# The seam between two layers: last rows in halves of tokens, a table fetched sooner, one W2 piece in a slot of its own

## The chip, the cores and the metric

The kernel runs on one core of a Trainium2 chip. TensorE (PE) multiplies, VectorE (DVE), ScalarE (ACT) and GpSimd (POOL) do the element-wise work, and the queues of SyncE (SP), ACT and POOL issue transfers to 16 DMA engines. The metric is the device time of one execution in microseconds (us).

## The reference

Two layers, each made of a spectral part A and a dense part B, both on a residual of 2048 tokens by 1024 features:

```python
x = A_x
x = x + _A_ref(_layernorm(x, axis=-1), A_w_r, A_w_i)
x = x + _B_ref(_layernorm(x, axis=-1), B_w1, B_b1, B_w2)
x = x + _A_ref(_layernorm(x, axis=-1), A_w_r, A_w_i)
x = x + _B_ref(_layernorm(x, axis=-1), B_w1, B_b1, B_w2)
```

`_A_ref` is a real 2-D FFT over tokens and features, a multiplication by the complex filter `w_r + i w_i`, and the inverse FFT. `_B_ref` is `act(x @ w1 + b1) @ w2` with 3584 hidden features and the activation h * tanh(softplus(h)), which ScalarE has as Mish.

## The kernel before, in words

Everything is written out by hand: each engine has its own list of instructions (`Prog`), in the order in which the Python code adds them, and each buffer (`Res`) remembers which counts of which semaphores its readers and writers must have reached. A transfer's waits are on the queue of the engine that issues it, so a waiting transfer holds back all that follows on that queue. On-chip memory is one big tensor, ARENA, in which `alloc` places named buffers at fixed offsets; a buffer laid over an older one inherits the older one's readers and writers as waits.

The residual stands in XS as 16 tiles j of 128 tokens. Layer A wants it in another order, XR: 128 rows, one for each (j, h) of token tile and feature block, each with 128 tokens n by 128 features. Its stages are: `s1` (L636), 16 groups of 8 matmuls, group j over tokens n = 8j to 8j + 7 of XR, each group read out of PSUM by ACT (L642) or DVE (L644) into Y; then by frequency group g = 0 to 7, in an order written out in `order_A`: `s2` (L726), `s3` (L771 to L774, then the filter's multiplications on DVE, L782 to L789, with the filter WT and the table FT), `i1` (L800, table BT), `i2` (L825). Tables FT and BT have rings of three buffers, filter groups a ring of eight buffers, two for each group. In layer 0 the filter is made and written to DRAM (`w_scratch`); in layer 1 it is read back by `load_w` on POOL's queue.

Layer B works by 512 hidden or output columns with a seven-product scheme. The second matmul of a pair of token blocks (`products`) has seven stages n, each with one block of W2 (or of sums of its blocks) and four token tiles t; a `tile_product` is 14 matmuls (L1309), seven for each of two pieces k of the W2 block. In the last pass of layer 0 the stages are in the order `BACK`, so that the residual's tiles become final one after the other in stages 4 and 6: (4, t) gives tile 12 + t, and (6, t) gives tile 8 + t. `turn_of` ends with (5,0), (5,1), (5,2), (6,0), (6,1), (6,2), (5,3), (6,3). W2 pieces are 896 KB and live in four slots R0 to R3:

```python
PB[n][k] = load_w2(stages[n][1], k, f"R{(2 * n + k + 1) % 4}")
```

They are loaded when stage n - 2 is over. So the two pieces of stage 6 (the block B21) take R1 and R2 after stage 4, while stage 5 uses R3 and R0.

At the seam each finished tile of the residual is normalised by DVE (L524) and goes to XR. All tiles but the last go by way of DRAM: `xn_store` on POOL's queue, `xr_load` on SP's. The last one, j = 11, is copied straight from the tile into XR by `xr_direct`, one copy for each of the eight feature blocks h, over the queues POOL, ACT, SP, POOL in turn. Meanwhile TensorE runs 38 filler matmuls (`spin`, L653). The residual's other data dependences at the seam are `r_xr`, two resources of 64 tokens each: `xr_load` and the whole-token `xr_direct` write both.

The next layer's tables and filter are opened by `open_tables(1)` ahead of `products`: filter groups 0 to 3, then FT and BT of groups 0 and 1, all on POOL's queue. The filter's eight buffers are the last 16 KB of ARENA. The slots WS0 to WS2 of the first matmul's weights end in the same place; WS2 is the last 7 KB.

Of the kernel before, what the change touches and what calls it, by code (L numbers as in the profile page):

```python
# [180 lines left out]
class KB:  # L181
# [185 lines left out]
    def layout(self):  # L367
        K = 1024
        self.o = dict(XR=0, Z=0, X=12 * K, T=20 * K, YK=28 * K, V=40 * K, JT=48 * K, M0=49 * K, IDF=49 * K + 256, RT=50 * K,
                      JUNK=51 * K, WR=54 * K, YS=96 * K, UT=64 * K, MN=64 * K, Y=96 * K, XN=128 * K, U=128 * K,  # L370
# [285 lines left out]
    def ring(self, name, n, size, shape):  # L656
        return [self.alloc(f"{name}{i}", self.o[name] + size * i, shape) for i in range(n)]

    def open_tables(self, li):

        self.li = li
        self.WT = self.ring("WT", 8, 2048, [2, 512])
        self.FTr = self.ring("FT", 3, 1536, [2, 384])
        self.BTr = self.ring("BT", 3, 1536, [2, 384])
        if li == 0:
            self.WR = self.ring("WR", 2, 4096, [2, 2, 512])
        for g in range(2 if li == 0 else 4):
            self.load_w(g)
        for g in range(2):
            self.load_tabs(g, li == 0)  # L670
            self.load_btabs(g, li == 0)

    def load_tabs(self, g, sp=False):
        b = self.FTr[g % 3]
        self.dma(self.sp if sp else self.pool, b.ap, self.con["FT"][g], f"ft{g % 3}{sp}", writes=[b.res])
# [10 lines left out]
        off = (self.o["WT"] + 2048 * i) // 2  # L686
        return self.ARENA[:, off:off + 2048].rearrange("p (a b c) -> p a b c", a=2, b=2)

    def load_w(self, g):
        if self.li == 0:  # L690
            self.load_wr(self.wr(g), g)
            return
        i = 2 * g % 8
        self.dma(self.pool, self.wt_pair(i), self.w_d[g], f"wt{g % 4}", reads=[self.r_wd[g]], writes=[w.res for w in self.WT[i:i + 2]])

    def layer_A(self, li):
        if li == 0:
# [6 lines left out]
        dve, act, sp, pool = self.dve, self.act, self.sp, self.pool  # L704
        ring, load_tabs, load_btabs, load_w = self.ring, self.load_tabs, self.load_btabs, self.load_w
        WT, FT, BT = self.WT, self.FTr, self.BTr
# [3 lines left out]
        def filter_bins(g):  # L710
            ps, banks, _ = self.pair()
            self.filter_bins(g, ps, banks, self.wr(g), WT[2 * g % 8:2 * g % 8 + 2], o["WT"] + 2048 * (2 * g % 8),
                             self.JT, self.r_jt, dve)

        def zslot(g, i):
            return Z[(2 * g + i) % 6]

        def s2(g, half):
# [14 lines left out]
            else:  # L733
# [16 lines left out]

            zz = self.ARENA[:, o["Z"] // 2 + (2 * g % 6) * K:o["Z"] // 2 + (2 * g % 6 + 2) * K].rearrange(
                "p (s r k) -> p s r k", s=2, r=2)
# [12 lines left out]
        def s3(g, i):  # L765

            ps, banks, _ = self.pair()
            z, ft = zslot(g, i), FT[g % 3]
            t = ft.ap[:, i, :]
            fns = [  # L770
                lambda e: e.matmul(ps[:, 0:512], t[:, 0:128], z.ap[:, 0, :], start=True, stop=False),  # L771
                lambda e: e.matmul(ps[:, 512:1024], t[:, 0:128], z.ap[:, 1, :], start=True, stop=False),
                lambda e: e.matmul(ps[:, 512:1024], t[:, 128:256], z.ap[:, 0, :], start=False, stop=True),
                lambda e: e.matmul(ps[:, 0:512], t[:, 256:384], z.ap[:, 1, :], start=False, stop=True),  # L774
            ]
            self.group(fns, reads=[z.res, ft.res], writes=banks)
            x = X[(2 * g + i) % 4]
            self.op(act, lambda e: e.activation(x.ap.rearrange("p a b -> p (a b)"), ps, ACT.Copy, scale=SIG),  # L778
                    reads=banks, writes=[x.res])
            wt, yk = WT[(2 * g + i) % 8], YK[(2 * g + i) % 6]  # L780
            ta, tb = T[2 * i], T[2 * i + 1]
            self.op(dve, lambda e: e.tensor_tensor(ta.ap, x.ap, wt.ap[:, 0:1, :].to_broadcast([P, 2, 512]), ALU.mult),  # L782
                    reads=[x.res, wt.res], writes=[ta.res])
            self.op(dve, lambda e: e.tensor_tensor(tb.ap, x.ap, wt.ap[:, 1:2, :].to_broadcast([P, 2, 512]), ALU.mult),
                    reads=[x.res, wt.res], writes=[tb.res])
            yk.res.begin()
            self.op(dve, lambda e: e.tensor_tensor(yk.ap[:, 0, :], ta.ap[:, 0, :], tb.ap[:, 1, :], ALU.subtract),
                    reads=[ta.res, tb.res], parts=[yk.res])
            self.op(dve, lambda e: e.tensor_tensor(yk.ap[:, 1, :], tb.ap[:, 0, :], ta.ap[:, 1, :], ALU.add),  # L789
                    reads=[ta.res, tb.res], parts=[yk.res])  # L790
# [117 lines left out]
                back((act, sp)[q % 2], 1, q, 1)  # L908

        self.s1(li)  # L910
        Z = ring("Z", 6, 2 * K, [2, 512])
        X = ring("X", 4, 2 * K, [2, 512])
        T = ring("T", 4, 2 * K, [2, 512])
# [8 lines left out]
        for stage, g, h in self.order_A():  # L922
            if stage == 2:
                s2(g, h)
                if li == 0 and h == 0:
                    filter_bins(g)
                    if g in (0, 1):
                        load_w(g + 4)
                    elif g in (4, 5):
                        load_w(g + 2)  # L930
            elif stage == 3:
                s3(g, h)
                if h:
                    if g < 6:
                        load_tabs(g + 2)
                    if li == 0:
                        self.keep_filter(g)
                    elif g < 4:
                        load_w(g + 4)
            elif stage == 4:  # L940
                i1(g, h)
                if h and g < 6:
                    load_btabs(g + 2)
            else:
                i2(g, h)
                u_turn(g, h)
# [160 lines left out]
    def layer_B(self, li, last):  # L1107
        pe, dve, act, sp, pool = self.pe, self.dve, self.act, self.sp, self.pool
# [164 lines left out]
        PB = [[None, None] for _ in range(7)]  # L1273
# [4 lines left out]
        def load_w2(name, k, slot, prog=sp):  # L1278

            b = self.alloc(f"W2{slot}", SLOT[slot], [7, 512])  # L1280
            f = slice(7 * k, 7 * k + 7)
            if name in T_OF:
                src, reads = self.w2s_d[T_OF[name]][:, f, :], [self.r_w2d[T_OF[name]][k]]
            else:
                d = 512 * int(name[2]) - 512
                src, reads = w2o[int(name[1]) - 1][:, f, d:d + 512], []
            self.dma(prog, b.ap, src, f"w2{slot}{prog.name}", reads=reads, writes=[b.res])
            return b

        STD = (("A11", "B11", 0, True), ("A12", "B21", 0, False), ("S", "T3", 1, True), ("A21", "T1", 0, True), ("A11", "T2", 1, True),  # L1290
               ("S", "B22", 0, False), ("A22", "T4", 1, False))
# [3 lines left out]
        def load_b(stages, n, k):  # L1295
            PB[n][k] = load_w2(stages[n][1], k, f"R{(2 * n + k + 1) % 4}")
# [20 lines left out]
        def products(p, s_off, stages, extra, loads=True):  # L1317
# [83 lines left out]
            for n, t in turn_of:  # L1401
                a, b, g, start = stages[n]
                bank = sets[g][t]
                if n or t:
                    tile_product(n, t, bank, ap[a], lambda k: part(a, k), start)
                after(b, t, bank)
                for f, k in sums.get((n, t), ()):
                    f(k)
                if t == 3 and n < 5 and loads:
                    for k in range(2):  # L1410
                        load_b(stages, n + 2, k)
                extra(n, t)

        self.xn_ring()
# [98 lines left out]
        gate = Res("gate")  # L1513
# [141 lines left out]
        stages = STD if last else BACK  # L1655
# [22 lines left out]
        def extra(n, t):  # L1678
            if last:
                return  # L1680
            if (n, t) == (2, 0):
                self.warm(ACT.Sqrt)
            if (n, t) == (3, 3):
                self.open_xr()
                for j in range(8):
                    self.xr_load(j)
            if n == 5 and t < 3:
                self.xr_load(12 + t)
            if (n, t) == (5, 2):
                self.xr_load(15)  # L1690
            if n in (4, 6):
                j = 4 * (n == 4) + 8 + t
                self.stats_second(j, 0, False)
                self.root(j, 1)
                b = self.apply(j, out=True)
                if j == 11:
                    self.xr_direct(j, b, 1, (pool, act, sp, pool))
                else:
                    self.xn_store(j, b)
            if n == 6 and t < 3:  # L1700
                if t:
                    self.xr_load(7 + t)
            if (n, t) == (5, 3):
                self.xr_load(10)
# [41 lines left out]
```

## Time and profile before

| | |
|---|---|
| median of three executions | 936.67 us (935.53 to 938.5) |
| profiled execution | 935.49 us, span 933.7 us |
| granted TensorE clock, mean | 0.993 |
| TensorE matmuls, busy share of the span | 94% |
| stage products and seam of layer 0 to 1 | about 397 to 500 us of the span |

Times in the views are microseconds from the start of the span. A line of the timeline gives the start, the length from the first to the last instruction of a run of equal ones, the engine, the source line, the operation with what it writes and reads, and the number of instructions; in square brackets, how long the engine stood idle before and what released it. A line of the waits gives the waiting engine and line, what it waited for, microseconds in total, the number of times, and the longest. The chain that ended last runs from the last instruction back through what released each step. "Issue" is time in which nothing that the profile shows was waited for. SPq, ACTq and POOLq are the queues' own work of issuing.

### The profile page before, as it was taken

What the parts mean: (1) busy time and instruction counts of PE and PEld (TensorE: products, weight loads), DVE (VectorE), ACT (ScalarE), POOL (GpSimd) and SP (SyncE); (2) the same over time, 40 slices, a digit from 0 to 9 for tenths busy, and PEclk for the clock granted to TensorE, in tenths of its full rate; (3) what the DMA queues carried; (4) which work ended last, traced back from release to release, by engine and by line L of the source; (5) the groups of instructions that cost most, each with busy time, mean ns of one, the idle gap of its engine ahead of it and who ended that gap; (6) DMA issues with size and microseconds to landing.
All of it is one profiled execution on the core that took longest, in us unless ns stands there. A gap on an engine that the chain in (4) does not pass through costs nothing.

```text
span 933.7 us, 13542 instructions
## 1 busy us (share of the span) xinstructions
PE 875.4 (94%) x5479; PEld 469.9 (50%) x5479; DVE 620.2 (66%) x985; ACT 434.4 (47%) x641; POOL 157.3 (17%) x181
## 2 busy tenths in 40 slices
PE   0699799999999999999999987999999999999998
PEld 0577486444444444444447765764444444444443
DVE  6698468687789667568756865666747665554473
ACT  6798485456213485420009975847650015552000
POOL 3923003960003641010120200000000000000000
PEclk9999989999999999999999998999999999999999
DMA  8969861674787388364830796445166635832432
GB/s 268 264 233 299 216 182 56 237 277 122 275 257 246 136 316 294 122 235 144 295 112 32 226 228 152 159 148 168 57 192 191 198 125 195 278 119 80 170 124 111
DMA packets 147392, 175.99 MB, mean 188 GB/s; under 512 B 68617, under 2 KB 125961, under 8 KB 147209
## 3 DMA queue, kind: packets, MB, share of 16 engines
q1 hardware_dynamic: 134656, 128.78, 44.7%
q0 software_dynamic: 10608, 44.70, 13.4%
q10 hardware_dynamic: 2064, 1.64, 0.6%
q8 instruction: 43, 0.70, 0.3%
q14 instruction: 21, 0.16, 0.1%
HBM read 130.78 MB, written 40.89 MB: 184 GB/s over the span
## 4 chain that ended last, share of the span: by engine, by line
PE 82%; DVE 6%; DMA 6%; ACT 4%; POOL 1%; issue 1%; SPq 1%; ACTq 0%; DVEq 0%; POOLq 0%
PE PS L1309 35%; PE PS L1210 29%; PE PS L1170 6%; PE PS L800 2%; PE PS L726 2%; PE PS L1021 2%; PE PS L825 2%; DMA XS<-in_A_x_dram 1%; DMA ARENA<-in_B_w_dram 1%; PE PS L1131 1%; DMA ARENA<-c_bt 1%; POOL ARENA L251 1%; DMA ARENA<-u_scratch 1%; DVE ARENA L644 1%; DMA u_scratch<-ARENA 1%; ACT ARENA L453 1%
## 5 line engine op out<-in xcount | busy, mean ns | idle before, releaser
L1309 PE MATMUL PS<-ARENA 128*128 128x512 bf16 x1568 | 340.4, 379 | 1.1 <-DMA ARENA<-in_B_w_dram 1.1
L1210 PE MATMUL PS<-ARENA 128*128 128x512 bf16 (+1 forms) x1288 | 280.3, 379 | 0.8 <-DVE ARENA L1215 0.8
L1309 PEld LDWEIGHTS PS<-ARENA 128*128 128x128 bf16 x1568 | 153.2, 98 | 186.2 <-DMA ARENA<-in_B_w_dram 1.1
L1215 DVE TENSOR_TENSOR ARENA<-PS,ARENA 128x512 f32<-128x512 f32 x230 | 157.0, 690 | 100.2 <-PE PS L1210 92.4
L1210 PEld LDWEIGHTS PS<-ARENA 128*128 128x128 bf16 x1288 | 125.4, 98 | 153.1 <-DVE ARENA L1215 3.5
L1220 ACT ACTIVATE ARENA<-ARENA,B 128x512 bf16<-128x512 f32 x138 | 98.8, 721 | 69.1 <-DVE ARENA L1215 63.8
L575 ACT ACTIVATE ARENA<-PS 128x512 f32<-128x512 f32 (+2 forms) x84 | 61.9, 741 | 115.0 <-PE PS L1210 92.5
L1103 POOL TENSOR_TENSOR ARENA<-ARENA 128x512 bf16<-128x512 bf16 x56 | 71.2, 1272 | 73.5 <-DVE ARENA L524 59.7
L453 ACT ACTIVATE ARENA<-XS 128x1024 bf16<-128x1024 bf16 x60 | 63.2, 1053 | 38.0 <-DVE XS L1360 33.0
L1170 PE MATMUL PS<-ARENA 128*128 128x256 bf16 (+1 forms) x528 | 73.4, 295 | 1.5 <-ACT ARENA L1174 1.4
L1334 DVE TENSOR_TENSOR ARENA<-ARENA 128x3584 bf16<-128x3584 bf16 x32 | 63.8, 2015 | 0.0
L1360 DVE TENSOR_TENSOR XS<-PS,ARENA 128x512 bf16<-128x512 f32 x52 | 35.7, 689 | 40.1 <-PE PS L1309 39.8
L1170 PEld LDWEIGHTS PS<-ARENA 128*128 128x128 bf16 x528 | 50.2, 98 | 20.3 <-ACT ARENA L1174 2.4
L1352 DVE TENSOR_TENSOR ARENA<-PS,ARENA 128x512 f32<-128x512 f32 x48 | 32.9, 687 | 27.6 <-PE PS L1309 27.1
L1174 ACT ACTIVATE ARENA<-PS,B 128x256 bf16<-128x256 f32 (+1 forms) x66 | 33.3, 515 | 29.1 <-PE PS L1170 28.8
L1220 ACT ACTIVATE ARENA<-PS,B 128x512 bf16<-128x512 f32 x46 | 31.5, 685 | 18.4 <-PE PS L1210 18.4
L1348 DVE TENSOR_TENSOR ARENA<-ARENA,XS 128x512 f32<-128x512 f32 x52 | 36.8, 731 | 0.5
L444 ACT ACTIVATE RS<-MV,EPS 128x1 f32<-128x1 f32 (+2 forms) x11 | 3.3, 296 | 72.2 <-DVE MV L566 71.6
L782 DVE TENSOR_TENSOR ARENA<-ARENA 128x1024 bf16<-128x1024 bf16 x32 | 22.0, 688 | 21.3 <-ACT ARENA L778 15.6
L800 PE MATMUL PS<-ARENA 128*128 128x256 bf16 x256 | 32.4, 273 | 3.9 <-DVE ARENA L789 3.2
L778 ACT ACTIVATE ARENA<-PS 128x1024 bf16<-128x1024 f32 x32 | 33.4, 1075 | 4.5 <-PE PS L774 4.5
L726 PE MATMUL PS<-FD,ARENA 128*128 128x256 bf16 (+1 forms) x256 | 31.8, 271 | 2.5 <-ACT ARENA L642 1.3
(97 smaller groups left out, 818.0 us busy)
## 6 DMA issues: line engine op xcount, KB each, us to landing
ARENA<-in_B_w_dram SPq DMA_DIRECT2D x30, 896.0 KB, 6.7
ARENA<-w1s_scratch SPq DMA_DIRECT2D x28, 896.0 KB, 4.6
ARENA<-w2s_scratch SPq DMA_DIRECT2D x24, 896.0 KB, 6.6
w1s_scratch<-ARENA POOLq DMA_DIRECT2D x14, 896.0 KB, 4.3
ARENA<-in_B_w_dram SPq DMA_DIRECT2D x24, 512.0 KB, 4.4
u_scratch<-ARENA SPq DMA_DIRECT2D x14, 512.0 KB, 3.5
ARENA<-u_scratch SPq DMA_DIRECT2D x14, 512.0 KB, 5.9
w2s_scratch<-ARENA POOLq DMA_DIRECT2D x8, 896.0 KB, 4.2
```

The source lines that it names most:

```text
L453: self.op(act, lambda e, i=i, f=f: e.activation(junk.ap, x, f, accum_out=sums[:, i:i + 1]), reads=[self.r_xs[j]], writes=[junk.res], parts ...
L575: fn = (lambda e: e.activation(dst, src, ACT.Copy)) if scale is None else \
L726: fns.append(lambda e: e.matmul(dst, at(r), FD[:, t:t + n], start=start, stop=stop))
L800: fns.append(lambda e, c=c, part=part: e.matmul(ps[:, c * 256:(c + 1) * 256], yk.ap[:, part, c * P:(c + 1) * P], t[:, (128, 0)[part]:(384, ...
L1103: self.op(self.pool, lambda e, dst=A(dst), x=A(x), y=A(y), op=op: e.tensor_tensor(dst, x, y, op), reads=[b.res] + list(after), writes=[b.rs])
L1170: fns.append(lambda e, db=db, bank=bank, fl=fl: e.matmul(PS[:, bank, 0:w], wb.ap[:, db, fl * P:(fl + 1) * P], x.ap[:, db, tok], start=(db ...
L1210: self.group([lambda e, db=db: e.matmul(PS[:, bank, :], A[:, db, :], mov[:, db, :], start=(start and db == 0), stop=(db == 3), skip_group_ ...
L1215: self.op(dve, lambda e: e.tensor_tensor(dst.ap, PS[:, bank, :], x.ap, ALU.add), reads=[self.r_bank[bank], x.res], writes=[dst.res])
L1220: self.op(act, lambda e: e.activation(at, src, ACT.Mish, bias=self.B1[:, ft:ft + 1]), reads=[res, self.r_b1], writes=[ra])
L1309: self.group([lambda e, i=i, k=k, b=PB[n][k].ap: e.matmul(PS[:, bank, :], ap[:, i, t * P:(t + 1) * P], b[:, i - 7 * k, :], start=(start an ...
L1334: self.op(dve, lambda e: e.tensor_tensor(ap[dst][:, f, :], ap[x][:, f, :], ap[y][:, f, :], op), reads=part(x, k) + part(y, k), writes=part ...
L1348: self.op(dve, lambda e: e.tensor_tensor(a[t], a[t], x, ALU.add), reads=[rx], writes=[r[t]])
```

## The change

Three things at the seam of the two layers, with a consequence for the filter.

- **Last rows in halves of tokens.** Tile 11's rows go to XR in two parts of 64 tokens, eight copies each, over eight queue places instead of four. The first part writes only the first of XR's two resources, so the first eight groups of `s1` no longer depend on the second part.
- **A table sooner.** `open_tables(1)` also loads FT of group 2, and the load in the loop at g = 0 goes. The order of the loads is now all FT, then all BT, in both layers.
- **A W2 piece in its own slot.** The first piece of stage 6 is loaded into Q3, which is the last 7 KB of ARENA, at (1, 0); only the second piece is still loaded at the end of stage 4. For this the filter's ring starts with four of its eight buffers in layer 1, and filter groups 2 and 3 are loaded after `s1` (`rest_of_filter`), behind a gate that holds what XR's writers and readers are.

```diff
-        self.WT = self.ring("WT", 8, 2048, [2, 512])
+        self.WT = self.ring("WT", 4 if li else 8, 2048, [2, 512])
...
-        for g in range(2 if li == 0 else 4):
+        for g in range(2):
             self.load_w(g)
+        for g in range(2 + li):
+            self.load_tabs(g, li == 0)
         for g in range(2):
-            self.load_tabs(g, li == 0)
             self.load_btabs(g, li == 0)
+
+    def rest_of_filter(self):
+
+        self.WT += [self.alloc(f"WT{i}", self.o["WT"] + 2048 * i, [2, 512]) for i in range(4, 8)]
+        gate = Res("gate")
+        for r in self.r_xr[1:3]:
+            gate.inherit(r)
+        for g in (2, 3):
+            self.load_w(g, [gate])
...
-    def load_w(self, g):
+    def load_w(self, g, after=()):
...
         self.s1(li)
+        if li:
+            self.rest_of_filter()
...
-                    if g < 6:
+                    if li <= g < 6:
                         load_tabs(g + 2)
...
                     for k in range(2):
-                        load_b(stages, n + 2, k)
+                        if stages is STD or (n, k) != (4, 0):
+                            load_b(stages, n + 2, k)
...
+            if (n, t) == (1, 0):
+                PB[6][0] = load_w2("B21", 0, "Q3")
...
                 if j == 11:
-                    self.xr_direct(j, b, 1, (pool, act, sp, pool))
+                    self.xr_direct(j, b, 2, (act, pool, sp, pool, sp, act, pool, sp))
```

More of the change, by code (lines that the diff above doesn't have):

```diff
@@ L693, in load_w @@
         i = 2 * g % 8
-        self.dma(self.pool, self.wt_pair(i), self.w_d[g], f"wt{g % 4}", reads=[self.r_wd[g]], writes=[w.res for w in self.WT[i:i + 2]])
+        self.dma(self.pool, self.wt_pair(i), self.w_d[g], f"wt{g % 4}", reads=[self.r_wd[g]] + list(after), writes=[w.res for w in self.WT[i:i + 2]])
     def layer_A(self, li):
```

## The prediction

> **What bounds the kernel now.** I read the page first (shares of busy time and the chain that ended last), then the waits of TensorE, then the chain and the timeline around the two places that the change names.
>
> ```profile
> PE 875.4 (94%) x5479; PEld 469.9 (50%) x5479; DVE 620.2 (66%) x985; ACT 434.4 (47%) x641; POOL 157.3 (17%) x181
> PE 82%; DVE 6%; DMA 6%; ACT 4%; POOL 1%; issue 1%; SPq 1%; ACTq 0%; DVEq 0%; POOLq 0%
> ```
>
> TensorE is 82% of the chain, and none of its matmuls is touched. All that the change can win is in the 6% of DMA, so I list what TensorE waited for and keep the two lines that belong to the change:
>
> ```profile
> PE PS L636 <- DMA ARENA<-ARENA: 1.5, 1, 1.5
> ...
> PE PS L1309 <- DMA ARENA<-in_B_w_dram: 1.1, 2, 0.6
> ```
>
> The first is the wait at the layers' seam (rows of the last token tile, copied straight into XR); the second the wait for the two pieces of W2 of the last product. The chain, in order of time, from that product to the next layer's first matmul:
>
> ```profile
> 454.33 11.80 DMA ARENA<-in_B_w_dram
> 466.13 0.05 issue
> 466.17 13.79 PE PS L1309 x63
> ...
> 483.45 5.36 DMA ARENA<-ARENA
> 488.81 0.82 issue
> ```
>
> Both transfers are links of the chain: what they lose, the run loses. The timeline gives the sizes:
>
> ```profile
> 461.69 1.67 PE L1309 MATMUL PS<-ARENA 128*128 128x512 bf16 x7
> 463.94 1.67 PE L1309 MATMUL PS<-ARENA 128*128 128x512 bf16 x7 [0.57 <-DMA ARENA<-in_B_w_dram]
> 479.78 8.36 PE L653 MATMUL PS<-BD 128*128 128x512 bf16 x38
> 482.85 1.19 SPq L251 DMA_DIRECT2D ARENA<-ARENA  x2
> 482.85 1.47 ACTq L251 DMA_DIRECT2D ARENA<-ARENA  x2
> 483.12 2.17 POOL L251 DMA_DIRECT2D ARENA<-ARENA  x4 [4.86 <-DVE ARENA L524]
> 485.28 0.54 POOL L251 DMA_DIRECT2D ARENA<-c_ft  x1
> 489.63 6.83 PE L636 MATMUL PS<-M,ARENA 128*128 128x128 bf16 x104 [1.48 <-DMA ARENA<-ARENA]
> ```
>
> The reader is to see a pair of short holes in front of stage 6 (seven matmuls, a hole, seven, a hole), then filler matmuls (L653, which compute nothing that is used) from 479.78 to 488.14, eight row copies issued over three queues, a table load right behind them on POOL's queue, and the first real matmul at 489.63.
>
> **What the Trainium skill says.** "DMA: Bandwidth & Descriptors", section "Anatomy of one DMA": a transfer has a fixed part of about 2 us, most of it the receipt of the last write, apart from the bytes. The trace agrees in kind: 32 KB row copies took 4.3 us (POOL, median) to 5.1 us (ACT, median) to land. The same page, "Queues, rings and completion order": each of the 16 DMA engines drains a ring in order and takes turns between the queues, so a copy on a new queue does not get round a busy engine. Its section "Why a DMA increments its semaphore by 16 and not by 1": only the full count means that all has landed, so the slowest engine decides. The two W2 pieces show this order: issued one after the other, they released TensorE at 463.94 and 466.17, 2.2 us apart.
>
> **The change part by part.**
>
> *W2 piece in its own slot.* Now both pieces of stage 6 (B21) are loaded at the end of stage 4, into slots R1 and R2, whose reader is stage 4 itself: issue at about 452.8 and 454.33, use after only three tiles of stage 5. In that stage a matmul is due every 30.22/140 = 0.216 us (the chain's row of 140), so seven take 1.51. Without waits the first half of tile (6,0) starts at 461.69 + 1.51 = 463.20 and the second at 464.71; they started at 463.94 and 466.17. Loss: 466.17 - 464.71 = 1.46 us. After the change piece 0 is loaded into Q3 some 50 us earlier. Piece 1 still cannot be issued before 454.33, since R2 is read until then; but piece 0 is no longer ahead of it, so it should land about 2.2 us sooner, at 463.9 where 464.71 is wanted. Margin 0.8 us: the wait goes, gain 1.46 us. If the backlog were more than I read, part stays; I put the lower end at 0.4. The early load itself is 0.9 MB on SP's queue behind the two pieces of stage 2, near 406. The stretches there have room:
>
> ```profile
> 410.00:413.00 3.00, 3.00 (x16) 1.36 (x14) 0.97 (x2) 0.00 (x0) 0.00 (x0) 1.00 0.54 225
> 413.00:416.00 3.00, 3.00 (x16) 1.35 (x15) 2.35 (x2) 0.00 (x0) 0.00 (x0) 1.00 0.00 0
> ```
>
> (the last two columns are DMA share and GB/s). Besides, two filter pieces of 512 KB are no longer loaded at 397 to 399. Cost nothing, and gain nothing either, as TensorE waits for no DMA there.
>
> *Rows in halves of tokens.* The first eight matmul groups of the next layer (L636) read tokens 0 to 63, the other eight tokens 64 to 127, but now all wait for eight copies of 128 tokens. After: sixteen copies of 64 tokens, the first eight (ACT 2, POOL 3, SP 3) release the first eight groups. Issue costs 2.17/4 = 0.54 us on POOL and 1.19/2 = 0.60 on SP. The last copy of POOL was issued at 483.12 + 3 x 0.54 = 484.74; the third, which ends the first half, at 484.20, and SP's third at 484.05. With the landing of 4.3 (POOL) and 4.7 (SP) that is 488.5 to 488.75, hardly better than before. But the landing falls too: on each DMA engine half the row bytes stand ahead, and the 192 KB table load behind them is gone. In the packets of the trace most engines were done with the rows by 486, and four engines, which still had the load of row 10's tile until 484.9, worked at the rows from then to 487.3. Half of 2.4 us is 1.2. I take 1.2 off the last release: landing at 488.0, TensorE 0.4 later at 488.4 (I leave the hand-over it had, last copy 489.2 to 489.63) instead of 489.63. Gain 1.2 us. Upper end 1.5, where the fillers end (488.14). Lower end 0.5: the shorter issue queue alone.
>
> Behind this stands the second half: six issues on POOL end at 483.12 + 3.26 = 486.4, on SP at 486.45, and with 4.3 to 5.4 us it lands at 490.7 to 491.8. The ninth group started at 493.82 in the trace and would start 1.2 sooner, 492.6. It waits for nothing. ACT issues four in place of two, until about 485.8; its first eviction after that was at 490.72.
>
> *Table sooner.* FT of group 2 moves from 485.28 to about 400, next to the other tables. Its gain is counted above. In layer 0 the same edit puts both FT ahead of both BT on SP; they are issued within 2 us of each other near 35, and BT's first user runs at 63. Nothing.
>
> *Filter groups 2 and 3 later.* Q3 lies where they were kept, so these 2 x 512 KB now come after the seam. Their wait is on XR's rows and on the last L636 matmul, at 498.2 - 2.7 = 495.5. Landing took 3.6 to 6.7 us, so both are there by 503.3; the first multiply with group 2 ran at 513.89, then 511.2. POOL, which waits, has nothing behind but loads first due at 508. Hidden, with 8 us to spare.
>
> *Sum.* 1.46 + 1.2 = 2.66 us of 936.67. One correction: the profiled execution took 935.49, 1.2 less than the median of the timed ones. If what varies is waits on DMA, these two waits are about a third of those TensorE shows (3.1 of 9 us without the start), so the usual run has some 0.4 more in them. That is a guess at the right order and adds 0.4 (0 to 0.8). 936.67 - 3.06 = 933.6.
>
> **The rivals.**
>
> *The seam's tail stays.* The four late DMA engines, not the bytes of the rows, set the landing, and the second half's packets push in among the first's. For it: the skill's turn-taking between queues; all 16 copies are in flight within 3.5 us. Against it: the first half is ahead on each queue. Gain 1.46 + 0.3: 934.9, not to be told from no change.
>
> *Piece 1 of W2 stays late.* Margin is only 0.8 us, and the load has to pass the row loads queued from 442 on. Then 0.4 of the 1.46 is won: 0.4 + 1.2 = 1.6, 935.1.
>
> *Slower.* The second half becomes the bound: six issues on the POOL queue could cost 0.89 each as its stores there do, ending 488.5, and if landing then takes twice 4.3 us, rows arrive at 497.1, 4.5 us after the ninth group's place. With the seam's gain of 1.2 lost in it and the 1.46 kept, that is 4.5 + 1.2 - 1.2 - 1.46 = +3.0: 939.7. Against it: the queues are otherwise empty then.
>
> **How the numbers follow.** Both waits gone 0.67, tail stays 0.14, piece late 0.10, slower 0.09. Of the first, gains run from 1.46 + 0.9 to 1.46 + 1.5 + 0.8; about 0.57 of the 0.67 lies over the bound of 0.3% (2.8 us), 0.10 under it. So faster 0.57, same 0.10 + 0.14 + 0.10 = 0.34, slower 0.09. Low end 932.2: full gains of 1.46 + 1.5 + 0.8 = 3.8 and 0.7 for the spread of the times. High end 936.4, a gain of almost nothing, which takes in both middle cases and leaves out the slower one.
>
> **What would show it.** Right: the row of waits L1309 on in_B_w gone; L636's wait on the row copies under 0.5 us or replaced by the fillers' end; the first L636 about 8.5 us after the last L1309 of the stage (9.7 now); no second wait between eighth and ninth group; filter loads landed before 505 with no wait at the multiplies. Wrong: a new wait of L636 in its middle, of the multiplies on w_scratch, or a seam that still takes 9.7 us.

## The result, and the profile after

The changed kernel took 932.46 us (median of six, 930.38 to 934.83), the kernel before 937.86 beside it: ratio 0.9946, 95% interval 0.9926 to 0.9966. Compared once more in the experiments the ratio was 0.9965 (0.9952 to 0.9978), that is 3.3 us (2.1 to 4.5). The forecast was 3.1.

L1309 of before is L1321 here, L771 is L781. The shares of the chain, from the page of the changed kernel:

```profile
PE 84%; DVE 4%; ACT 4%; SPq 4%; DMA 3%; issue 1%; POOL 0%; ACTq 0%; DVEq 0%
```

DMA has gone from 6% to 3%. (Of these shares only a part belongs to the seam: in this execution the start of the run hangs on SP's issue queue and not on a transfer.) The chain of the changed kernel over the same stretch:

```profile
460.19 10.74 PE PS L1321 x49
470.93 0.05 issue
470.99 9.44 PE PS L1321 x43
480.43 1.29 PE PS L653 x6
481.72 0.05 issue
481.78 6.85 PE PS L653 x31
488.63 0.46 PE PS L636 x8
```

Both links of DMA are gone, and in the list of TensorE's waits neither of the two rows of before is left. The products run without a hole, and what leads to the first L636 is now the filler matmuls of L653. The timeline (start, length, engine, line, operation, number) shows it directly:

```profile
480.27 8.37 PE L653 MATMUL PS<-BD 128*128 128x512 bf16 x37
483.34 3.73 SPq L251 DMA_DIRECT2D ARENA<-ARENA  x6
483.34 2.76 ACTq L251 DMA_DIRECT2D ARENA<-ARENA  x4
488.47 6.83 PE L636 MATMUL PS<-M,ARENA 128*128 128x128 bf16 x104
```

The last line has no bracket of idle time: TensorE goes from the fillers into L636, and between the eighth and the ninth group (16 groups of L636, the second eight on the second half of the rows) it waits for no rows either. How the sixteen copies themselves went (duration of an issue, first and last start, and over all transfers of that stretch the time to landing):

```profile
L251 SPq DMA_DIRECT2D ARENA<-ARENA x6: 539/592/598, 483.3 to 486.5; - x6
L251 POOL DMA_DIRECT2D ARENA<-ARENA x6: 529/529/586, 483.6 to 486.3; - x6
L251 ACTq DMA_DIRECT2D ARENA<-ARENA x4: 552/630/858, 483.3 to 485.5; - x4
...
DMA to landing us min/median/max: 2.1/2.4/2.8
```

An issue costs about what it did (medians 0.53 us on POOL, 0.59 on SP, 0.63 on ACT), but a copy lands in 2.4 us where the same view of the kernel before, with its table load among the transfers, says:

```profile
DMA to landing us min/median/max: 3.9/4.3/5.4
```

Two lengths serve for all that follows, both from starts of matmuls in the trace: the **pass**, from the first to the last L1309 of the last product pass of layer 0, and the **seam**, from that last L1309 to the first L636 of layer 1. Before: pass 87.59, seam 10.06 us. After: 86.12 and 8.42. (The prediction counted the seam from the end of that L1309: its 9.7 and 8.5 are 10.06 and 8.83 here.) The sum of the two differences is 1.47 + 1.64 = 3.11 us. The spans of this one pair of profiles differ by only 0.7, because in the profiled execution of the changed kernel layer 0 happened to reach this pass 1.95 us later, and the stretch behind the first L636 took 0.5 longer; its time, 934.83, is the longest of its six.

### The profile page after: what moved, and what is told of

It is laid out like the page before. It is cut to its first block, busy times and chain, and to the rows that moved or that the text cites. A ratio compares the mean times of both kernels' runs of the same rounds, so it can differ in the third digit from the quotient of the medians.

```text
span 933.0 us, 13477 instructions
## 1 busy us (share of the span) xinstructions
PE 870.8 (93%) x5404; PEld 470.5 (50%) x5479; DVE 620.8 (67%) x985; ACT 434.8 (47%) x641; POOL 158.9 (17%) x183
## 3 DMA queue, kind: packets, MB, share of 16 engines
q10 hardware_dynamic: 2096, 1.64, 0.6%
## 4 chain that ended last, share of the span: by engine, by line
PE 84%; DVE 4%; ACT 4%; SPq 4%; DMA 3%; issue 1%; POOL 0%; ACTq 0%; DVEq 0%
PE PS L1321 36%; PE PS L1222 29%; PE PS L1182 6%; SPq L251 4%; PE PS L810 2%; PE PS L736 2%; PE PS L1033 2%; PE PS L835 2%; PE PS L1143 1%; DMA ARENA<-c_bt 1%; DMA ARENA<-u_scratch 1%; PE PS L653 1%; DMA u_scratch<-ARENA 1%; ACT ARENA L453 1%; DVE ARENA L792 1%
## 5 line engine op out<-in xcount | busy, mean ns | idle before, releaser
L1321 PE MATMUL PS<-ARENA 128*128 128x512 bf16 x1535 | 338.2, 379 | 1.7
L1222 PE MATMUL PS<-ARENA 128*128 128x512 f16 (+1 forms) x1265 | 279.0, 379 | 2.0 <-DVE ARENA L1227 0.8
L1321 PEld LDWEIGHTS PS<-ARENA 128*128 128x128 bf16 x1568 | 153.4, 98 | 184.4
```

Source lines behind the costliest of these rows:

```text
L1222: self.group([lambda e, db=db: e.matmul(PS[:, bank, :], A[:, db, :], mov[:, db, :], start=(start and db == 0), stop=(db == 3), skip_group_ ...
L1321: self.group([lambda e, i=i, k=k, b=PB[n][k].ap: e.matmul(PS[:, bank, :], ap[:, i, t * P:(t + 1) * P], b[:, i - 7 * k, :], start=(start an ...
```

## The experiments

The changed kernel's first comparison, the same kernel again and eleven others, each beside runs of the kernel before on the same chip. The last column is how long after the last L1309 all rows of tile 11 had landed (for halves of tokens: first half, then all). Pass, seam and landing come from one profiled execution of each kernel.

| kernel | ratio (95% interval) | pass | seam | rows landed |
|---|---|---|---|---|
| before | | 87.59 | 10.06 | 9.65 |
| changed | 0.9946 (0.9926 to 0.9966) | 86.12 | 8.42 | 7.03, 8.58 |
| after_again | 0.9965 (0.9952 to 0.9978) | 86.12 | 8.42 | 7.06, 8.58 |
| only_w2 | 0.9974 (0.9964 to 0.9984) | 86.12 | 11.36 | 10.95 |
| only_halves | 0.9992 (0.9984 to 1.0001) | 88.31 | 8.42 | 7.46, 8.86 |
| only_table | 0.9998 (0.9987 to 1.0009) | 87.50 | 10.15 | 9.73 |
| only_l0 | 1.0004 (0.9994 to 1.0013) | 87.71 | 10.22 | 9.81 |
| w2_halves | 0.9956 (0.9939 to 0.9972) | 86.12 | 8.42 | 6.95, 8.60 |
| after_spin31 | 0.9956 (0.9943 to 0.9969) | 86.13 | 7.66 | 7.31, 8.93 |
| after_spin26 | 0.9956 (0.9943 to 0.9970) | 86.12 | 7.32 | 6.98, 8.66 |
| after_joined | 0.9971 (0.9960 to 0.9982) | 86.12 | 9.13 | 7.08, 8.68 |
| before_row10 | 1.0001 (0.9990 to 1.0011) | 87.43 | 10.13 | 9.73 |
| before_queues | 0.9995 (0.9986 to 1.0004) | 87.65 | 10.47 | 10.12 |
| before_features | 0.9999 (0.9987 to 1.0010) | 87.43 | 11.31 | 11.11 |

### The change in parts

Theory: two waits go, worth 3.1 us together. Rivals: something elsewhere is faster too, or one of the small edits carries the gain.

**only_w2**: the kernel before with the ring of four, `rest_of_filter` and

```diff
+            if (n, t) == (1, 0):
+                PB[6][0] = load_w2("B21", 0, "Q3")
```

> Only the W2 piece in Q3 with what it needs (filter ring of four, groups 2 and 3 after s1); rows whole, tables as before. Theory (two waits at the seam, 1.5 us and 1.6 us, are all that the change removes; anything over 3.1 us in the medians is spread between executions): last product pass 1.5 us shorter than before (first to last L1309 matmul 86.1 in place of 87.6), seam as before (9.9 to 10.1 us from the last L1309 to the first L636), 0.15% faster. Rival (the rearranged transfers save time elsewhere too): 0.3% or more faster.

The pass is 86.12, as forecast. Its time gained 0.26%, 2.4 us (1.5 to 3.4), somewhat over the 1.5 of the pass. In the one profiled execution the seam was longer than before, 11.36: the rows landed late, and TensorE, idle for 2.8 us, began at half pace (last section). So the profile shows nothing that would explain a gain over 1.5. (Its span is 1.6 us shorter than that of before: 2.1 by an earlier arrival at the pass and 1.47 by the pass, less 1.3 at the seam and 0.7 behind it. The arrival varies by 4 us between the profiles of this study, so the 2.1 is no sign of a gain elsewhere.) The rest stays open, and so does whether the rows were late by chance or by the moved loads.

**only_halves**:

```diff
-                    self.xr_direct(j, b, 1, (pool, act, sp, pool))
+                    self.xr_direct(j, b, 2, (act, pool, sp, pool, sp, act, pool, sp))
```

> Only tile 11's rows in halves; W2 piece, filter and tables as before. Theory: pass as before (87.6 us), seam down to 8.4 us where the fillers end, or up to 9.0 with the table load still behind the rows; 0.1 to 0.17% faster. Rival (the row 10 load that was still under way on four DMA engines sets the landing, and halves don't change that): seam 9.5 us or more, no change of time.

Seam 8.42, at the fillers' end, with the table load still on POOL's queue. The pass was 88.31 in this execution: the wait for W2 varies. The time gained 0.08%, 0.7 us, less than the 1.6 of the seam, and the interval (1.5 us faster to 0.1 slower) reaches past zero: the seam is shown by the trace alone. The two parts together, 0.26% and 0.08%, make 0.34%, as much as after_again gained; each has an interval of about 0.1% to either side, so how they share it is not shown by time.

**only_table** and **only_l0**: FT of group 2 in layer 1's `open_tables`; and both FT ahead of both BT in layer 0 alone.

```diff
+        if li:
+            self.load_tabs(2)
...
-                    if g < 6:
+                    if li <= g < 6:
                         load_tabs(g + 2)
```

> Only FT of group 2 loaded with the other tables in layer 1; layer 0's order untouched. Theory: the table's packets come after the rows on each engine, so the rows land at most 0.5 us sooner: seam 9.4 to 10.1 us, no change that can be told. Rival (the table load is what held the rows up): seam 8.6 us or less, 0.15% faster.

> Only layer 0's order of the first table loads (both FT ahead of both BT), as the change has it. Theory: no change, under 0.1%. Rival (the part of the gain over 3.1 us comes from layer 0): about 0.2% faster, and layer 0's first i4 matmul sooner by 1 to 2 us.

Neither does anything: ratios at 1, seams 10.15 and 10.22, rows landed as before. In layer 0 the first matmul of `i4` (L1021, the last stage of A's inverse transform) was at 113.96 us with the new order and 114.44 with the old; over all profiles of this study it lay between 112.82 and 116.17 with the new order and between 111.88 and 114.78 with the old.

**w2_halves** is the change without its tables:

> The change without its table part: W2 piece in Q3 and rows in halves; FT of group 2 is loaded in the loop, and tables alternate as before. Theory (the table load plays no part): pass 86.1 us, seam 8.4 us, no new wait of s3 for FT, 0.25 to 0.45% faster than before, as the changed kernel. Rival (with rows and filter loads on the same queue the table comes too late, or its early load is a part of the gain): a wait of L771's kind on c_ft, or 0.1% less gain.

Pass, seam and time are those of the changed kernel, and `s3` waits for no FT. The table part plays no role that these runs show, alone or in company.

**after_again**:

> The changed kernel once more, beside the same runs of before as the next three. Theory (1.5 us at stage 6, 1.6 us at the seam, both as an execution with little waiting shows them, and more in the usual one): 0.30 to 0.45% faster, pass 86.1 us, seam 8.4 us. Rival (its first comparison, 0.54% on six runs a side, is the effect): 0.5% or more.

3.3 us (2.1 to 4.5), pass and seam to the hundredth of a us as in the first profile. So 3.1 is inside. The 5.1 of the first comparison (3.2 to 6.9) is above it; the two intervals overlap between 3.2 and 4.5, and w2_halves, with 4.1, lies there.

### What now sets the first L636

**after_spin31, after_spin26**: `self.spin(38, 7)` with 31 or 26.

> The changed kernel with 31 filler matmuls in place of 38. Theory (after the change the fillers' end at 8.4 us, not the rows, sets the first L636; the first half of the rows had landed at 6.7 to 7.5 us after the last L1309 of the pass): seam 7.2 to 7.9 us, 0.05 to 0.12% faster than the changed kernel. Rival (the rows land later in most executions, or the clock falls when TensorE idles): seam 8.4 us or more, or the first groups at half pace, no gain.

> The changed kernel with 26 fillers, which end about 5.8 us after the last L1309. Theory: the rows' landing sets the start, so the seam is that of 31 fillers (7.2 to 7.9 us) and the time the same. Rival (the idle time lets the clock fall): first groups of L636 slower than 0.45 us apart, no gain over 38 fillers or a loss.

The timeline of after_spin26:

```profile
477.60 5.78 PE L653 MATMUL PS<-BD 128*128 128x512 bf16 x26
484.70 3.51 PE L636 MATMUL PS<-M,ARENA 128*128 128x128 bf16 x53 [1.33 <-DMA ARENA<-ARENA]
```

The bracket is back: with the fillers out of the way the rows' first half is what L636 waits for, and it starts 0.3 to 0.4 us after they landed (6.98, then 7.32). So after the change the fillers had been the bound, by 0.8 to 1.1 us. The clock holds (first groups 0.45 us apart). Both kernels have a median 1.4 us under that of after_again; their intervals overlap with its own, so by time alone the further gain is not told apart, though the seams show it. They have the lowest medians of this study, 931.36 and 931.44 us.

### Why the half copies land sooner

I had put it to the bytes ahead on four busy engines and to the table load behind them. Four kernels, each with one thing changed.

**before_row10**: no load of tile 10's rows under way while tile 11's are copied.

```diff
-                if j == 11:
+                if j in (10, 11):
                     self.xr_direct(j, b, 1, (pool, act, sp, pool))
...
-            if (n, t) == (5, 3):
-                self.xr_load(10)
```

> The kernel before, with tile 10's rows also copied straight into XR (whole, eight copies, the same queues) in place of the way through DRAM, so that no load of row 10 is under way when tile 11's rows are copied. Theory (that load, still busy on some DMA engines, held up tile 11's rows): the rows land about 7 to 8 us after the last L1309 in place of 9.7, the seam is 8.4 us where the fillers end, 0.1 to 0.17% faster. Rival (the number and size of the row copies set the landing): seam 9.5 us or more, no change.

Landed at 9.73, seam 10.13: no change. My theory fell. The trace's records of single packets show why it had looked right. Without the load of row 10 the packets of the eight copies were over sooner, at 5.33 (SP), 6.07 (ACT) and 6.98 us (POOL) after the last L1309, in place of 7.49, 7.78 and 8.06 before. But the last landing of each queue was at 8.89, 9.34 and 9.73, where before it was at 9.04, 9.24 and 9.65. So the end of the packets, from which I had read the delay, does not set the landing of whole copies. (The load of row 9 is issued later here, but its data were in place before the first copy of tile 11 began.)

**before_queues**: whole copies on the change's queues.

> The kernel before with whole copies of tile 11's rows, but over the change's queues: ACT 2, POOL 3, SP 3 in place of POOL 4, ACT 2, SP 2. Theory (the size of the copies, not their queues, makes them land late): last landing 9.2 to 9.8 us after the last L1309, seam 9.6 to 10.2, no change of time. Rival (the fourth copy on POOL's queue is what is late): landing 8.7 us or less, seam 9.1 or less, 0.1% faster.

10.12 and 10.47, later than forecast and not better than before: it isn't the fourth copy on POOL's queue.

**after_joined**: half copies, but `res = self.r_xr[1:3]` for both halves, so that L636 waits for all sixteen.

> The changed kernel, sixteen half copies as they are, but all of them written to both of XR's resources, so that the first L636 waits for all sixteen. Theory (the half copies land sooner as such, all by 8.6 us): seam 8.9 to 9.1 us, so of the 1.7 us at the seam about 1.1 come from the copies' form and 0.6 from the split wait; 0.25 to 0.3% faster than before. Rival (the split wait is the gain): seam 9.6 us or more.

```profile
479.46 8.37 PE L653 MATMUL PS<-BD 128*128 128x512 bf16 x37
488.38 3.79 PE L636 MATMUL PS<-M,ARENA 128*128 128x128 bf16 x58 [0.55 <-DMA ARENA<-ARENA]
```

Seam 9.13: with the split wait taken away, more than half of the seam's gain is still there (0.93 of 1.64 us). All sixteen half copies, with twice the issues, have landed by 8.68, a whole us ahead of eight whole ones.

**before_features**: sixteen copies of half the features of all 128 tokens, 16 KB each as the halves of tokens are.

```diff
-                self.dma(prog, self.XR.ap[row_of(j, h):row_of(j, h) + 1, n, :], b.ap[n, h * P:(h + 1) * P], f"xd{j}{k}{prog.name}",
+                self.dma(prog, self.XR.ap[row_of(j, h):row_of(j, h) + 1, n, f:f + 64], b.ap[n, h * P + f:h * P + f + 64], f"xd{j}{k}{prog.name}",
```

> The kernel before with tile 11's rows in sixteen copies of all 128 tokens by half the features of a block (16 KB, pieces of 128 bytes), on the change's queues; the first L636 waits for all. Tells what of the half copies makes them land sooner. If the bytes of a copy: landing by 8.6 to 9.0 us after the last L1309, seam 9.0 to 9.4. If the token rows (pieces) of a copy: landing 9.7 us or later, seam 10.1 or more, since each copy still has 128 pieces and there are twice as many.

The landing in the stretch of the copies:

```profile
DMA to landing us min/median/max: 2.8/4.7/5.3
```

The same bytes a copy as the halves of tokens, but 128 pieces from 128 tokens, and in the median it lands like a whole copy. In before_queues, whole copies and the table load:

```profile
DMA to landing us min/median/max: 4.6/5.2/5.9
```

and in after_joined, half copies:

```profile
DMA to landing us min/median/max: 2.2/2.5/2.8
```

So fewer bytes in a copy (16 KB both times) are not enough, and the queue and the neighbours were not it. The number of token rows in a copy, 64 or 128, fits all these views, but it is not shown alone. before_features also has twice as many pieces in all, 2048 of 128 bytes in place of 1024 of 256, and its first copies on SP and POOL landed in 2.8 and 3.3 us, the other fourteen in 4.3 to 5.3: pieces that pile up would look like this too. It is one execution besides, and not a usual one: by time the kernel is as fast as before (0.9999), though this profile is 1.25 us longer at the seam. Copies of 64 rows by half the features, or other counts of rows, would separate the two; I did not try them. What in the transfer makes copies of 128 rows land later stays open.

## Why the prediction was right

The chain was read rightly: two transfers on it, both gone, 3.11 us in the pair of profiles and 3.3 (2.1 to 4.5) in the second comparison, where the text said 3.06. Of that 3.06, 1.46 was right in its reason, 1.2 came near for a wrong reason, which is luck, and 0.4 was a guess. By its steps:

- **W2 piece.** Forecast 1.46, pass shorter by 1.47. Seven profiles with the old slots have passes of 87.43 to 88.31, mean 87.66; seven with Q3 have 86.12 or 86.13. The piece that is still loaded late had a forecast margin of 0.8 us. The view of the W2 loads of the changed kernel around it:

```profile
DMA to landing us min/median/max: 4.9/7.0/9.8
```

  The longest is that piece: issued at 456.29, landed at 466.09, used at 466.67. It took 9.8 us in place of 11.8, so it came 2.0 us sooner where 2.2 was forecast. Margin 0.58 here. In the seven profiles the load took 9.1 to 10.3 us and the margin was 0.05 (after_spin31) to 1.25: it held in all seven, once at the very edge.
- **Rows in halves.** Forecast 1.2, measured 1.64: the term was too small. The landing of the first half was put at 488.0, which is 8.4 us after the last L1309, and was at 7.03; the fillers' end, at 8.42, cut the gain. The text had that end as its upper bound, but put it at 1.5: it took the recorded end of the last filler, and L636 starts a little before it. The reason behind the number was wrong: "half of 2.4 us", four engines busy with tile 10's load. before_row10 shows that load to play no part in the last landing (9.73 without it, 9.65 with it). What changed was the landing time of a copy, which I had taken over from the whole copies (4.3 to 4.7): in halves it fell to 2.4.
- **Second half.** Forecast at 490.7 to 491.8, wanted at 492.6. In the terms of the kernel before it landed at 479.57 + 8.58 = 488.2, for the same reason. No stall, as said.
- **Table.** Its removal was part of the forecast relief; it gave nothing (only_table, w2_halves).
- **Filter groups 2 and 3.** Forecast hidden, landed before 505. The timeline of the changed kernel has them issued behind the last L636 group; they landed at 500.96 and 502.25, and the view of their tensor has no waiter:

```profile
497.38 1.12 POOL L251 DMA_DIRECT2D ARENA<-w_scratch  x2 [10.55 <-PE PS L636]
```

- **The 0.4 us for the usual run.** Not shown. Passes of before average 0.07 over the one I read, seams with whole copies (only_w2's 11.36 left aside) 10.06 to 10.47, 0.15 over it on average: some 0.2 where 0.4 was added. With the 11.36 counted in, the seams are 0.34 over it and the sum is 0.4. One late execution decides, so the profiles are too few. The text's "3.1 of 9 us" was misread besides: the two waits in its own lines are 1.5 and 1.1, so 2.6.

Of the rivals, "the seam's tail stays" and "slower" needed late rows, which came early. The sum of "slower" was wrong as well: rows at 497.1 are 3.3 us after the ninth group's old place at 493.82, and less 1.46 that is +1.8, 938.5; the text took the distance from the forecast place, 492.6, as a loss against the kernel before. "Piece 1 of W2 stays late" missed by 0.58 us in the changed kernel's profile and by 0.05 in that of after_spin31.

## What to carry to other kernels

When a transfer stands on the chain between two products, look first at which buffer its issue waits for: a piece that could lie somewhere else until then took its whole wait out of the pass (1.47 us), and no run showed a cost for moving it. The margin of the piece that stayed is then worth a look in more than one profile: here it ran from 0.05 to 1.25 us. When the wait in front of a stage is cut, look at what else fills that time; here filler work became the bound, and shortening it showed 0.8 to 1.1 us more in the trace. Try a copy in two forms before reasoning about its neighbours: here the form of the copies did what queue, table and traffic had been thought to do.

## What the runs showed of the hardware

Copies from 128 or from 64 token rows into one row of XR: 64 rows landed in 2.1 to 2.8 us in the changed kernel, 128 rows in medians of 4.3 (before) to 5.2 (before_queues), and 4.7 at half the bytes but twice the pieces (before_features). The Trainium skill, "DMA: Bandwidth & Descriptors", "Anatomy of one DMA", gives for a transfer from GpSimd (POOL) about 2.0 us plus bytes over 436 GB/s; estimated from it, 32 KB should land in 2.1 us and 16 KB in 2.0. The half copies, at 2.1 to 2.8, are near it; for 128 rows the measurement is twice that and decides.

TensorE's pace after a wait. In only_w2 it stood idle for 2.8 us behind the fillers; its stretches (length, busy times, then the granted clock, DMA share, GB/s):

```profile
487.00:488.50 1.50, 1.14 (x12) 1.17 (x13) 0.09 (x1) 0.00 (x0) 0.00 (x0) 0.57 0.00 0
488.50:490.00 1.50, 1.50 (x17) 1.50 (x16) 1.14 (x1) 0.74 (x1) 0.00 (x0) 0.50 0.00 0
490.00:491.50 1.50, 1.50 (x24) 1.50 (x23) 1.38 (x2) 0.90 (x2) 0.00 (x0) 0.79 0.00 0
491.50:494.00 2.50, 2.44 (x42) 2.11 (x40) 2.19 (x2) 2.50 (x4) 0.00 (x0) 1.00 0.00 0
```

The first four groups of L636 came 0.81 to 0.85 us apart in place of 0.45, and layer 1's first L726 started 11.1 us after the first L636 in place of 9.9. before_features, idle for 2.7 us, fell to 0.50 as well, some 1.1 us into L636, and lost the same 1.2 us. After 1.3 to 1.9 us of idle time at this place (after_spin26 1.33, before 1.48, before_queues 1.89) the first groups kept their 0.45 us. The Trainium skill, "TensorE: Matmul & The Clock Gate", "What's actually happening", has the array at half clock after an idle window of about 3.4 us; here shorter times without a matmul, 2.7 and 2.8 us, were followed by it, and 1.9 us was not.
